# A chunked recurrence with two MLPs behind it: a set order for VectorE, full-height products placed by DMA, relu squared on ScalarE

## The chip, the cores and the metric

The kernel runs on one NeuronCore of a Trainium2 chip. The metric is device time of one execution in microseconds; the median of several executions counts. TensorE (PE) multiplies matrices into PSUM, VectorE (DVE), ScalarE (ACT) and GpSimd (POOL) work elementwise, and SyncE (SP) issues most of the DMAs. Each engine works through its own instructions in order and waits on semaphores for the others.

## What is computed

Three parts follow each other. First a recurrence over 768 steps for 4 batches of 8 heads with a 40 x 40 state each; then a dense MLP whose activation is relu squared; then a mixture of 8 experts with one expert per token. All in float32. The cores of the first two:

```python
for t in range(S):
    y[:, :, t] = np.einsum('bhd,bhde->bhe', rt, state)
    Sa = np.einsum('bhde,bhe->bhd', state, at)
    state_decay = state * wt[:, :, None, :] - np.einsum('bhd,bhe->bhde', Sa, bt)
    state = state_decay + np.einsum('bhd,bhe->bhde', vt, kt)

h = x @ w_in
r = np.maximum(h, 0.0)
g = r * r
return (g @ w_out).astype(np.float32)
```

The third part takes the argmax of x @ w_gate for each token, gives the token to that expert's relu MLP (320 to 1024 to 320) and scales by the softmax weight.

## The kernel before, in words

The 768 steps are cut into 12 superchunks of 64 (index s), each of two chunks of 32 (index c). Inside a chunk the recurrence is turned into matrix products and the inverse of unit lower triangular 32 x 32 matrices. The MLP of a superchunk (a "burst", 8 pieces fp of up product, activation and down product) is cut into pieces that are laid between the recurrence's steps, so that TensorE has something to do while the recurrence waits for other engines. The experts come last, from about 800 us on.

What a superchunk needs is made ahead. `scale` (line 143) loads the decays w and the operands k, b and a of a superchunk, and `products` (line 115) forms running products of w: r by a backward scan (line 126), a clamp (line 135) after ScalarE has looked at the range (line 133), a reciprocal seed, and q by a forward scan (line 139). kb is multiplied by r (line 158) and a by q (through `times`, line 283). The scans exist twice: 104 rows and 1040 columns for operands with the head's columns on partitions (buffers w_d and rq16), and 128 rows and 650 columns in `steps` (line 230, buffers wl and rq10) for operands with the steps on partitions. Both share one seed buffer, seed_q. `by_step` transposes r and q into rt and qt.

`lower` (line 175) makes the products pa of a and kb; ScalarE copies one half to ab (line 186), VectorE masks the other half to am (line 188) and transposes it into a (line 192). `invert` (line 195) transposes ab to al (line 199), and then GpSimd alone works through 31 dependent pairs of a product and a subtraction (line 290: tmp, then tl). tmp shares its one buffer with am. `inverted` (line 215) transposes tl to tf and makes tt from it, which `solve` needs in the next superchunk.

A chunk runs through slots (lines 1430 to 1484): slot_a `out` of the chunk before (products py, and y by VectorE, line 389; ScalarE doubles the last 64 columns, line 390) and `right` (pr); slot_b `add_y` (line 463 and 464: y transposed by TensorE to pt and split into x_hi, x_lo, x_mx for the MLP), `solve` (psa, with ScalarE's copies to sa and zv), in the first chunk of a superchunk also `lower` and `invert` for the superchunk after, and the transposes pz of `other`; slot_d the transposes psd and the products ppq; slot_e, in the first chunk, `steps` of the next superchunk; slot_f `mix`, in the first chunk `decay` of the operands of the next superchunk (line 349), and `fetch`, the loads for the next chunk and the product of zk with rx (line 283); slot_g the update pn of the state (line 307). After each slot MLP pieces are taken, as many as `SLOTS` says: 18 in the first chunk, 14 in the second. `up` (line 647) makes relu on ScalarE (line 654), its square gh on ScalarE (line 658), and on VectorE the product of pl and g (line 659) and the rest gl (line 660). The down product reads gh and gl two pieces later.

A planner orders each engine's instructions from this program order, a timing model and priorities, and so may draw an instruction ahead whose inputs are there. `issue_after` sets an order by hand on one engine; `behind` puts VectorE's instructions behind the last state update in that way. Tiles of a tag share its buffers: rx and the range check's output share one, al and tf share one (solve).

Of the kernel before, what the change touches and what calls it, by code (L numbers as in the profile page):

```python
# [28 lines left out]
SC = 64  # L29
NS = S // SC  # L30
C = 32
# [41 lines left out]
class Rwkv:  # L73
# [6 lines left out]
    def __init__(self, ctx, tc, ps, consts, keep, wd, kb, ad, rv, wl, tok, vt, rng, cst):  # L80
# [28 lines left out]
        self.sums = []  # L109
# [8 lines left out]
    def products(self, w, n, rows, name):  # L118
# [16 lines left out]
        nc.vector.tensor_scalar(out=rf, in0=rf, scalar1=1.0 / LIM, scalar2=LIM, op0=ALU.max, op1=ALU.min)  # L135
        nc.vector.reciprocal(out=self.sq[:rows, 0:n, 0], in_=r[:rows, :, 0])
        yield r
        q = self.tile([128, n, SEG], f"rq{n}.q{name}", 1)
        nc.vector.tensor_tensor_scan(out=q.rearrange("p a b -> p (a b)")[:rows], data0=w[:rows, 0:L],  # L139
                                     data1=seed,  # L140
                                     initial=0.0, op0=ALU.mult, op1=ALU.add)
        yield q

    def scale(self, s):

        nc, src = self.nc, self.src
        w, kb, a = self.w, self.kb, self.a[s % 2]
# [1206 lines left out]
def tile_rwkv__mlp__moe(ctx, tc, wd, kb, ad, rv, wl, tok, vt, nat, w_in, w_out, w_gate, w1, w2, cap, cst1, cst2, cst3, out):  # L1354
# [9 lines left out]
    with ExitStack() as ph:  # L1364
# [24 lines left out]
        with tc.high_priority(offset=AHEAD):  # L1389
# [3 lines left out]
            for _ in rw.scale(1):  # L1393
                pass
# [225 lines left out]
```

## Time and profile before

| | |
|---|---|
| median of 3 executions | 1119.45 us (1116.76 to 1121.55) |
| the profiled execution | 1115.53 us, of it 1113.7 us from the first to the last instruction |
| TensorE, weight loads | 906.6 and 854.7 us busy |
| VectorE | 848.5 us busy |
| ScalarE | 565.9 us busy |
| GpSimd | 510.4 us busy |
[...]

Busy time is not progress: matmuls overlap, and a slow clock makes the same matmuls longer. The busy sums are averages over the load of the weights (up to about 220 us), the superchunks, and the experts. In the rows below, a line such as "POOL tmp <- DVE a L192" names the waiting instruction's output and line first, then what ended the wait. A group "x9 | 6.1, 680 | 8.1 <-ACT gh" has the count, the busy microseconds, the mean of one in nanoseconds, and the idle time ahead of it.

### The profile page before, as it was taken

Reading aid. Unit: us, or ns where it says so; the run is one execution under the profiler, and the core shown is the slowest. Engines: PE = TensorE matmul, PEld = TensorE weight load, DVE = VectorE, ACT = ScalarE, POOL = GpSimd, SP = SyncE. Lnnn points to the kernel's source line nnn. Section 1 sums busy time; section 2 is a strip of 40 time slices with the busy share of each in tenths; the row PEclk is TensorE's granted clock in tenths of the full one; section 3 lists DMA queues with packets and bytes.
Section 4 is the critical chain, followed back from the end, with each engine's and each line's share of the span. In section 5 each row is a group of like instructions: output and inputs, shape, how many; then the busy total and the mean of one; then the engine's idle time right before and its main releaser. Section 6 shows DMA issues by size and latency. Waiting matters only on the chain.

```text
span 1113.7 us, 38734 instructions
## 1 busy us (share of the span) xinstructions
PE 906.6 (81%) x15962; PEld 854.7 (77%) x15962; DVE 848.5 (76%) x1807; ACT 565.9 (51%) x1546; POOL 510.4 (46%) x866
## 2 busy tenths in 40 slices
PE   1645348798898988898979888999899998999992
PEld 1544337688787878887969787899799998989992
DVE  7978888687787877978777878764777878778860
ACT  2434435454544544545454545555273667767750
POOL 4692763848383828284746557540000132223220
PEclk9755558888999989898998999999899999999997
DMA  8833544854444444454535444343294576768720
GB/s 212 252 92 102 153 113 118 275 137 129 116 135 134 134 129 132 123 151 106 156 103 141 121 132 136 103 125 83 74 315 117 160 224 195 224 199 237 216 81 9
DMA packets 86111, 164.18 MB, mean 147 GB/s; under 512 B 15709, under 2 KB 46047, under 8 KB 84960
## 3 DMA queue, kind: packets, MB, share of 16 engines
q1 hardware_dynamic: 76848, 141.52, 45.1%
q10 hardware_dynamic: 6192, 11.06, 3.6%
q0 software_dynamic: 2880, 8.98, 2.5%
q8 instruction: 129, 2.11, 0.9%
q14 instruction: 62, 0.51, 0.2%
HBM read 137.34 MB, written 16.24 MB: 138 GB/s over the span
## 4 chain that ended last, share of the span: by engine, by line
PE 40%; DVE 18%; DMA 12%; POOL 11%; issue 10%; ACT 3%; SPq 0%; POOLq 0%; DVEq 0%; ACTq 0%
PE pl L448 12%; PE acc L632 11%; DMA out_dram<-uo,room 6%; POOL tl L290 5%; POOL tmp L290 5%; DMA xg<-x_dram,room 3%; PE upl L448 3%; PE uacc L1142 3%; PE ppq L293 2%; DVE rq_r L126 2%; PE pn L293 2%; DVE a L283 2%; DVE rq_q L139 1%; DVE zk L283 1%; PE psa L293 1%
## 5 line engine op out<-in xcount | busy, mean ns | idle before, releaser
L290 POOL TENSOR_TENSOR tmp<-solve_al,tl 128x126 f32<-128x126 f32 (+22 forms) x372 | 188.1, 506 | 211.3 <-DVE a L192 183.1
L290 POOL TENSOR_TENSOR tl<-tl,tmp 128x126 f32<-128x126 f32 (+22 forms) x372 | 220.0, 592 | 29.1
L632 PE MATMUL acc<-woh,gh 128*128 128x328 f32 x384 | 129.5, 343 | 2.3 <-ACT x L685 1.9
L659 DVE TENSOR_TENSOR g<-pl,g 128x512 f32<-128x512 f32 x96 | 65.6, 684 | 84.5 <-ACT gh L658 83.6
L448 PE MATMUL pl<-x_hi,wi_hi 128*128 128x256 f32 x384 | 122.3, 318 | 6.5 <-DVE g L659 3.4
L632 PE MATMUL acc<-wol,gh 128*128 128x328 f32 x384 | 123.0, 326 | 0.0
L448 PE MATMUL pl<-x_lo,wi_hi 128*128 128x256 f32 x384 | 115.6, 301 | 8.1 <-DVE x_lo L463 8.1
L448 PE MATMUL pl<-x_hi,wi_lo 128*128 128x256 f32 x384 | 114.6, 298 | 0.0
L654 ACT ACTIVATE g<-pl 128x512 f32<-128x512 f32 x96 | 57.4, 598 | 94.7 <-PE pl L448 93.6
L1220 POOL DMA_INDIRECT out_dram<-uo,room x30 | 34.1, 1137 | 149.9 <-DVE uo L1209 82.4
L1150 POOL DMA_INDIRECT xg<-x_dram,room x30 | 30.7, 1022 | 147.1 <-DVE room L982 66.7
L632 PE MATMUL acc<-woh,gl 128*128 128x328 f32 x384 | 92.4, 323 | 0.0
L448 PEld LDWEIGHTS pl<-x_hi,wi_hi 128*128 128x128 f32 x384 | 79.8, 208 | 10.0 <-DVE g L659 3.5
L448 PEld LDWEIGHTS pl<-x_lo,wi_hi 128*128 128x128 f32 x384 | 80.5, 210 | 8.4 <-DVE x_lo L463 8.4
L1142 PE MATMUL uacc<-w2h,hh 128*128 128x320 f32 x240 | 76.6, 319 | 9.6 <-DVE uo L1209 9.4
L632 PEld LDWEIGHTS acc<-woh,gh 128*128 128x128 f32 x384 | 76.4, 199 | 4.9 <-ACT x L685 2.2
L448 PEld LDWEIGHTS pl<-x_hi,wi_lo 128*128 128x128 f32 x384 | 80.0, 208 | 0.0
L632 PEld LDWEIGHTS acc<-wol,gh 128*128 128x128 f32 x384 | 76.9, 200 | 0.5 <-issue 0.5
L1142 PE MATMUL uacc<-w2h,hl 128*128 128x320 f32 x240 | 75.0, 312 | 0.0
L1142 PE MATMUL uacc<-w2l,hh 128*128 128x320 f32 x240 | 74.9, 312 | 0.0
L403 ACT COPY zk<-pz 40x160 f32<-40x160 f32 x184 | 52.8, 287 | 34.3 <-PE pz L271 31.6
L660 DVE TENSOR_TENSOR gl<-g,gh 128x512 fp32r<-128x512 f32 x96 | 67.9, 707 | 1.8
(266 smaller groups left out, 2716.3 us busy)
## 6 DMA issues: line engine op xcount, KB each, us to landing
wol<-wol SPq DMA_DIRECT2D x96, 328.0 KB
w<-in_w_dram SPq DMA_DIRECT2D x30, 640.0 KB
w<-in_w_dram SPq DMA_DIRECT2D x30, 512.0 KB
zv<-in_vt_dram SPq DMA_DIRECT2D x48, 208.0 KB
kb_d<-in_kb_dram SPq DMA_DIRECT2D x24, 320.0 KB
zk<-in_tok_dram SPq DMA_DIRECT2D x48, 160.0 KB
rx<-rt SPq DMA_DIRECT2D x192, 40.0 KB
w<-in_w_dram SPq DMA_DIRECT2D x30, 256.0 KB
```

What stands on the lines that cost most here:

```text
L283: self.nc.vector.tensor_tensor(op=ALU.mult, **k)
L290: self.last = f(*a, **k).ins
L293: self.tc.keep_in_program_order(self.nc.tensor.matmul(*a, **k))
L403: self.nc.scalar.copy(v[:, y], pz[j][one(y)[1]])
L448: tc.keep_in_program_order(tc.nc.tensor.matmul(out, lhsT=a, rhs=b, start=n == 0, stop=n == len(seq) - 1))
L632: self.tc.keep_in_program_order(self.nc.tensor.matmul(*a, **k))
L654: nc.scalar.activation(g, pl, AF.Relu)
L659: nc.vector.tensor_tensor(out=g, in0=pl, in1=g, op=ALU.mult)
L660: self.behind = (square, nc.vector.tensor_tensor(out=gl, in0=g, in1=gh.bitcast(F32), op=ALU.subtract).ins)
L1142: self.tc.keep_in_program_order(self.nc.tensor.matmul(*a, **k))
L1150: nc.gpsimd.indirect_dma_start(out=xg[:, 0:DX], out_offset=None, in_=self.x1, in_offset=bass.IndirectOffsetOnAxis(ap=self.idx[2 * j + t], ...
L1220: self.nc.gpsimd.indirect_dma_start(out=self.out, out_offset=bass.IndirectOffsetOnAxis(ap=self.to[:, n:n + 1], axis=0), in_=o[:, t], in_of ...
```

## The change

- `up`: ScalarE squares relu in place into g and copies it to gh; VectorE's product of pl and g goes.
- The a operand is loaded into one tile of 104 rows, ax, that shares rq16's one buffer with r; it is multiplied by q in one product of 104 rows, read there by pa, and copied into the two halves of a by DMAs on SP (`place`), the second chunk at once and the first after its decay, which is one product of 104 rows too.
- k and b by steps are loaded into a tile tk of 128 rows in `fetch`; `ready`, in slot_b of the next chunk, multiplies it by rx in one product, and two DMAs place the halves in zk.
- The q scans write over w instead of a buffer of their own. The clamp comes ahead of the range check, whose limits move to 2/LIM and LIM/2.
- `gated` puts VectorE's instructions behind those listed in `gate`: the last one of `add_y` (x_mx), and from `invert` on al. It holds for the r scans of both kinds, am, the product in `ready` and the decay of a, from superchunk 2 on (`steady`).
- In `scale` the products start two slots later; am and its transposes move to `put`, after `invert`.
- tmp has a buffer of its own. ab shares one with sad instead.
- The doubled last 64 columns of y are made by a second VectorE product from py instead of ScalarE's copy from y.

```diff
+        nc.vector.tensor_scalar(out=rf, in0=rf, scalar1=1.0 / LIM, scalar2=LIM, op0=ALU.max, op1=ALU.min)
         if n == 10:
             s = name
 
                 over = self.tile([128, n, SEG], f"over.{s}_{k}", 1, tag="rx")
                 nc.scalar.activation(over, r, AF.Relu,
                                      bias=self.c["lim"][:, k:k + 1], scale=sign, accum_out=self.rng[:, k, s:s + 1])
-        nc.vector.tensor_scalar(out=rf, in0=rf, scalar1=1.0 / LIM, scalar2=LIM, op0=ALU.max, op1=ALU.min)
         nc.vector.reciprocal(out=self.sq[:rows, 0:n, 0], in_=r[:rows, :, 0])
         yield r
-        q = self.tile([128, n, SEG], f"rq{n}.q{name}", 1)
-        nc.vector.tensor_tensor_scan(out=q.rearrange("p a b -> p (a b)")[:rows], data0=w[:rows, 0:L],
-                                     data1=seed,
+        q = w[:, 0:L]
+        nc.vector.tensor_tensor_scan(out=q[:rows], data0=q[:rows], data1=seed,
                                      initial=0.0, op0=ALU.mult, op1=ALU.add)
-        yield q
+        yield q.rearrange("p (a b) -> p a b", a=n)
...
     def scale(self, s):
 
         nc, src = self.nc, self.src
-        w, kb, a = self.w, self.kb, self.a[s % 2]
+        w, kb = self.w, self.kb
         for j in range(2):
             nc.sync.dma_start(out=w[BY_COL[j]], in_=src["wd"][s, j])
         for j in range(2):
             nc.sync.dma_start(out=kb[BY_COL[j]], in_=src["kb"][s, j])
 
+        yield
+        yield
         pr = self.products(w, 16, ROWS, s)
-        r = next(pr)
+        with self.gated():
+            r = next(pr)
         yield
         for k in range(2):
             with self.behind(2):
                 nc.vector.tensor_mul(kb[:ROWS, k], kb[:ROWS, k], r[:ROWS, :, 1:SEG])
-            yield
+        yield
         g = self.tile([128, 16], f"g64.{s}", 2)
         nc.vector.tensor_copy(g[:ROWS], r[:ROWS, :, 0])
         self.pre[s] = [g, [None] * NC, None]
-        for j in range(2):
-            nc.sync.dma_start(out=a[BY_COL[j], :, j].rearrange("p c n t -> p c (n t)"), in_=src["ad"][s, j])
+        x = self.tile([128, NC, 16, C], f"rq16.a{s}", 1)
+        nc.sync.dma_start(out=x[:ROWS].rearrange("p c n t -> p (c n t)"), in_=src["ad"][s])
         q = next(pr)
-        yield
-        for j in range(2):
-            v = a[BY_COL[j], :, j]
-            with self.behind(2):
-                self.times(s > 0 or j == 0, out=v, in0=v, in1=q[BY_COL[j], :, 0:SC].rearrange("p n (c t) -> p c n t", c=NC))
+        with self.behind(2):
+            nc.vector.tensor_tensor(out=x[:ROWS], in0=x[:ROWS], in1=q[:ROWS, :, 0:SC].rearrange("p n (c t) -> p c n t", c=NC),
+                                    op=ALU.mult)
+        self.ax = x
+        self.place(s, 1)
         self.wl = self.tile([128, 1 + 10 * SEG], f"wl.{s}", 1)
         nc.sync.dma_start(out=self.wl, in_=src["wl"][s])
         yield
 
+    def place(self, s, c):
+
+        for j in range(2):
+            self.nc.sync.dma_start(out=self.a[s % 2][BY_COL[j], c, j], in_=self.ax[BY_COL[j], c])
+
     def lower(self, s, c):
         kb, a = self.kb, self.a[s % 2][:, c]
+        if s == 0 and c == 0:
+            self.place(s, 0)
         if c == 0:
-            self.ab = self.tile([128, C, NC, H], f"ab.{s}", 1)
+            self.ab = self.tile([128, C, NC, H], f"sad.ab{s}", 1)
         pa = self.psum(f"pa{s}_{c}").rearrange("p (h k s) -> p h k s", h=H, k=2)
         t0 = c * C
         for h, b, i, lane, ty, j in heads():
             rows = BY_COL[j]
-            self.mm(pa[lane, h], lhsT=a[rows, j, i], rhs=kb[rows, :, i, t0:t0 + C], start=True, stop=True)
+            self.mm(pa[lane, h], lhsT=self.ax[rows, c, i], rhs=kb[rows, :, i, t0:t0 + C], start=True, stop=True)
         nc.scalar.copy(self.ab[:, :, c, :], pa[:, :, 1, :].rearrange("p h s -> p s h"))
+        self.todo.append((s, c, a, pa))
+
+    def put(self):
+
+        nc = self.nc
+        s, c, a, pa = self.todo.pop(0)
         am = self.tile([128, H, C], f"am.{s}_{c}", 1)
-        nc.vector.tensor_tensor(out=am, in0=pa[:, :, 0, :], in1=self.c["mlow"][:, None, :].to_broadcast([128, H, C]),
-                                op=ALU.mult)
+        with self.gated():
+            nc.vector.tensor_tensor(out=am, in0=pa[:, :, 0, :], in1=self.c["mlow"][:, None, :].to_broadcast([128, H, C]),
+                                    op=ALU.mult)
         for j in range(2):
             ak = a[BY_STEP[j], j].rearrange("p (h y) t -> p y h t", y=2)
             nc.vector.transpose(out=ak[:, 0], in_=am[BY_STEP[j]])
...
+        i = nc.vector.transpose(out=al.rearrange("p s t -> p (s t)"), in_=self.ab.rearrange("p s c h -> p s (c h)")[:, :, None].to_broadcast([128, C, 2, NC * H]))
+        self.gate = [i.ins]
         tl = self.tile([128, C, C // 2], f"tl.{s}", 1)
-        tmp = self.tile([128, 144], f"tmp.{s}", 1, tag="am")
+        tmp = self.tile([128, 144], f"tmp.{s}", 1)
...
     def steps(self, s):
 
         pr = self.products(self.wl, 10, 128, s)
-        r = next(pr)
+        with self.gated():
+            r = next(pr)
         yield
...
-        for j in range(2):
-            nc.sync.dma_start(out=zk[BY_STEP[j], j], in_=src["tok"][s, c, j])
+        tk = self.tile([128, 16, D], f"tk.{s}_{c}", 1)
+        nc.sync.dma_start(out=tk.rearrange("p n e -> p (n e)"), in_=src["tok"][s, c])
...
+        self.got.append((zk, tk, rx))
+
+    def ready(self):
+
+        nc = self.nc
+        if not self.got:
+            return
+        zk, tk, rx = self.got.pop(0)
+        v = tk.rearrange("p (h y) e -> p y h e", y=2)
+        with self.gated():
+            nc.vector.tensor_tensor(out=v, in0=v, in1=rx, op=ALU.mult)
         for j in range(2):
-            v = zk[BY_STEP[j], j].rearrange("p (h y) e -> p y h e", y=2)
-            self.times(c == 1 or s > 0, out=v, in0=v, in1=rx[BY_STEP[j]])
+            nc.sync.dma_start(out=zk[BY_STEP[j], j], in_=tk[BY_STEP[j]])
...
+    def gated(self):
+
+        order = ExitStack()
+        for i in self.gate if self.steady else ():
             order.enter_context(self.tc.issue_after(i))
...
     def decay(self, s):
 
-        g = self.pre[s][0]
-        for z in (self.a[s % 2][:, 0], self.zv[0]):
-            for j in range(2):
-                v, w = z[BY_COL[j], j], g[BY_COL[j], :, None].to_broadcast([D, 16, C])
-                if z is self.zv[0]:
-                    v = each(v)
-                    w = g[BY_COL[j]].rearrange("p (n y) -> p n y", y=2)[:, :, :, None].to_broadcast([D, 8, 2, D])
-                self.nc.vector.tensor_mul(v, v, w)
-            yield
+        g, x = self.pre[s][0], self.ax[:ROWS, 0]
+        with self.gated():
+            self.nc.vector.tensor_mul(x, x, g[:ROWS, :, None].to_broadcast([ROWS, 16, C]))
+        self.place(s, 0)
+        yield
...
+        self.nc.vector.tensor_mul(y[:, 0:DM], py, q)
+        self.nc.vector.tensor_mul(y[:, DM:], py[:, DM - 64:], q[:, DM - 64:])
...
-        square = nc.scalar.activation(gh, g, AF.Square).ins
-        nc.vector.tensor_tensor(out=g, in0=pl, in1=g, op=ALU.mult)
-        self.behind = (square, nc.vector.tensor_tensor(out=gl, in0=g, in1=gh.bitcast(F32), op=ALU.subtract).ins)
+        nc.scalar.activation(g, g, AF.Square)
+        self.behind = (nc.scalar.copy(gh, g).ins, nc.vector.tensor_tensor(out=gl, in0=g, in1=gh.bitcast(F32), op=ALU.subtract).ins)
...
-        lim=np.broadcast_to([[1.0 / LIM, -LIM]], (128, 2)),
+        lim=np.broadcast_to([[2.0 / LIM, -LIM / 2]], (128, 2)),
...
-                        ml.add_y(xs[last[0]], last[1], y)
+                        rw.gate = [ml.add_y(xs[last[0]], last[1], y).ins]
...
+                        rw.put()
+                        rw.put()
                     if c == 0 and s > 0:
                         next(decay)
                     others(0)
+                    rw.ready()
...
+                rw.steady = s > 1
```

Left out: the host's layouts of a and of k and b by steps (now 104 and 128 rows in one piece), returned instructions, a renamed tag for a late tile of the experts, and the calls of `put` and `ready` for superchunk 0.

## Rows read from the trace of the kernel before

**Rows 1.** Busy time by stretch: length, then PE, PEld, DVE, ACT, POOL, clock, DMA.

```profile
222.00:281.00 59.00, 53.38 (x1158) 49.69 (x1158) 49.54 (x80) 29.88 (x75) 38.55 (x68) 0.86 0.47 128
...
637.00:696.00 59.00, 50.28 (x1166) 47.01 (x1166) 47.15 (x78) 29.18 (x73) 34.71 (x65) 0.94 0.51 140
696.00:745.00 49.00, 47.03 (x1153) 44.21 (x1153) 32.87 (x60) 27.29 (x68) 26.20 (x62) 0.97 0.41 112
745.00:793.00 48.00, 47.72 (x1004) 45.35 (x1000) 29.32 (x75) 24.85 (x62) 0.00 (x0) 1.00 0.28 80
```

**Rows 2.** Who waited for whom: us in total, times, longest.

```profile
POOL tmp L290 <- DVE a L192: 183.1, 12, 21.6
...
PE psd L271 <- DVE x_mx L464: 26.0, 9, 4.1
...
PE pz L271 <- DVE x_mx L464: 20.5, 8, 3.7
...
DVE rq_r L135 <- ACT over L133: 19.7, 10, 2.4
```

**Rows 3.** Timeline of VectorE at one superchunk's head: start, length.

```profile
398.48 0.48 DVE L389 TENSOR_TENSOR y<-py,qt 128x320 f32<-128x320 f32 x1
398.88 2.31 DVE L126 TENSOR_TENSOR_SCAN rq_r<-w_d,seed_q 104x1040 f32<-104x1040 f32 x1
...
406.50 0.27 DVE L464 TENSOR_TENSOR x_mx<-pt,tops 64x128 fp32r<-64x128 f32 x1
...
408.62 1.23 DVE L199 STREAM_TRANSPOSE solve_al<-ab 128x1024 f32<-128x1024 f32 x1
```

**Rows 4.** Busy time by stretch, right behind that head.

```profile
407.00:413.00 6.00, 6.00 (x30) 5.92 (x29) 5.83 (x13) 3.33 (x9) 0.00 (x0) 0.51 0.63 148
```

**Rows 5.** Timeline of GpSimd: two inversions, first and last steps, one slow step.

```profile
413.32 0.24 POOL L290 TENSOR_TENSOR tmp<-solve_al,tl 128x31 f32<-128x31 f32 x1 [17.95 <-DVE a L192]
...
427.78 3.56 POOL L290 TENSOR_TENSOR tl<-tl,tmp 128x128 f32<-128x128 f32 x1
...
450.96 0.22 POOL L290 TENSOR_TENSOR tl<-tl,tmp 128x16 f32<-128x16 f32 x1
...
706.54 0.24 POOL L290 TENSOR_TENSOR tmp<-solve_al,tl 128x31 f32<-128x31 f32 x1 [13.92 <-DVE a L192]
...
737.29 0.22 POOL L290 TENSOR_TENSOR tl<-tl,tmp 128x16 f32<-128x16 f32 x1
```

**Rows 6.** VectorE's groups in superchunk 5 (398 to 459 us).

```profile
L659 DVE TENSOR_TENSOR g<-pl,g 128x512 f32<-128x512 f32 x9 | 6.1, 680 | 8.1 <-ACT gh L658 8.0
...
L283 DVE TENSOR_TENSOR zk<-zk,rx 64x640 f32<-64x640 f32 x4 | 3.4, 847 | 1.7 <-DMA zk<-in_tok_dram 1.6
...
L283 DVE TENSOR_TENSOR a<-a,rq_q 40x1024 f32<-40x1024 f32 x2 | 2.7, 1338 | 0.0
L158 DVE TENSOR_TENSOR kb_d<-kb_d,rq_r 104x1024 f32<-104x1024 f32 x2 | 2.3, 1208 | 0.0
...
L349 DVE TENSOR_TENSOR a<-a,g 40x512 f32<-40x512 f32 x2 | 1.4, 686 | 0.0
```

**Rows 7.** ScalarE's group of squares in superchunk 5.

```profile
L658 ACT ACTIVATE gh<-g 128x512 fp32r<-128x512 f32 x8 | 5.0, 630 | 0.2
```

**Rows 8.** The chain that ended last, two DMA pieces: start, length.

```profile
253.81 3.59 DMA a<-in_ad_dram
...
390.39 4.68 DMA rx<-rt
```

**Rows 9.** Timeline: al and GpSimd's first step, first and third inversion.

```profile
33.85 1.24 DVE L199 STREAM_TRANSPOSE solve_al<-ab 128x1024 f32<-128x1024 f32 x1
...
38.34 2.52 POOL L290 TENSOR_TENSOR tmp<-solve_al,tl 128x31 f32<-128x31 f32 x1 [1.72 <-DVE a L192]
...
179.63 1.24 DVE L199 STREAM_TRANSPOSE solve_al<-ab 128x1024 f32<-128x1024 f32 x1
...
182.74 0.24 POOL L290 TENSOR_TENSOR tmp<-solve_al,tl 128x31 f32<-128x31 f32 x1 [21.57 <-DVE a L192]
```

More of the change, by code (lines that the diff above doesn't have):

```diff
@@ L108, in __init__ @@
         self.last = None
-        self.sums = []
+        self.todo, self.got = [], []
+        self.sums, self.gate, self.steady = [], [], False
         self.pre, self.rt = {}, {}
@@ L198, in invert @@
         al = self.tile([128, C, C], f"solve.al{s}", 1)
-        nc.vector.transpose(out=al.rearrange("p s t -> p (s t)"), in_=self.ab.rearrange("p s c h -> p s (c h)")[:, :, None].to_broadcast([128, C, 2, NC * H]))
+        i = nc.vector.transpose(out=al.rearrange("p s t -> p (s t)"), in_=self.ab.rearrange("p s c h -> p s (c h)")[:, :, None].to_broadcast([128, C, 2, NC * H]))
+        self.gate = [i.ins]
         tl = self.tile([128, C, C // 2], f"tl.{s}", 1)
-        tmp = self.tile([128, 144], f"tmp.{s}", 1, tag="am")
+        tmp = self.tile([128, 144], f"tmp.{s}", 1)
         eng, pin = nc.gpsimd, self.pool
@@ L276, in behind @@
         for i in self.sums[:n]:
+            order.enter_context(self.tc.issue_after(i))
+        return order
+    def gated(self):
+        order = ExitStack()
+        for i in self.gate if self.steady else ():
             order.enter_context(self.tc.issue_after(i))
@@ L340, in decay @@
     def decay(self, s):
-        g = self.pre[s][0]
-        for z in (self.a[s % 2][:, 0], self.zv[0]):
-            for j in range(2):
-                v, w = z[BY_COL[j], j], g[BY_COL[j], :, None].to_broadcast([D, 16, C])
-                if z is self.zv[0]:
-                    v = each(v)
-                    w = g[BY_COL[j]].rearrange("p (n y) -> p n y", y=2)[:, :, :, None].to_broadcast([D, 8, 2, D])
-                self.nc.vector.tensor_mul(v, v, w)
-            yield
+        g, x = self.pre[s][0], self.ax[:ROWS, 0]
[3 more added lines that the diff above has]
+        yield
+        for j in range(2):
+            v = each(self.zv[0][BY_COL[j], j])
+            w = g[BY_COL[j]].rearrange("p (n y) -> p n y", y=2)[:, :, :, None].to_broadcast([D, 8, 2, D])
+            self.nc.vector.tensor_mul(v, v, w)
+        yield
     def turn(self, s, c):
@@ L382, in out @@
     def out(self, s, c):
-        py = self.psum(f"py{s}_{c}")[:, 0:DM].rearrange("p (h e) -> p h e", h=H)
+        py = self.psum(f"py{s}_{c}")[:, 0:DM]
+        ph = py.rearrange("p (h e) -> p h e", h=H)
         for h, b, i, lane, ty, j in heads():
             rows = BOTH[j]
-            self.mm(py[lane, h], lhsT=self.lr[c][rows, j, i], rhs=self.zk[c][rows, j, i], start=True, stop=True)
+            self.mm(ph[lane, h], lhsT=self.lr[c][rows, j, i], rhs=self.zk[c][rows, j, i], start=True, stop=True)
         y = self.tile([128, DM + 64], f"y.{s}_{c}", 1)
-        self.nc.vector.tensor_mul(y[:, 0:DM].rearrange("p (h e) -> p h e", h=H), py, self.pre[s][1][c])
-        self.nc.scalar.copy(y[:, DM:], y[:, DM - 64:DM])
+        q = self.pre[s][1][c].rearrange("p h e -> p (h e)")
+        self.nc.vector.tensor_mul(y[:, 0:DM], py, q)
+        self.nc.vector.tensor_mul(y[:, DM:], py[:, DM - 64:], q[:, DM - 64:])
         return y
@@ L1020, in early @@
         nb, n = 2 * FIRST_UNITS, 2 * NE
-        op = [rw.tile([128, m, 128], f"{t}.op{m}", 1, dt=F32R) for t, m in (("solve", 8), ("rq16", 8), ("ab", n - 16))]
+        op = [rw.tile([128, m, 128], f"{t}.op{m}", 1, dt=F32R) for t, m in (("solve", 8), ("rq16", 8), ("sad", n - 16))]
         ov = rw.tile([128, n, nb], "rq10.ov", 1, dt=F32R)
@@ L1448, in slot_b @@
                         rw.invert(s + 1)
+                        rw.put()
+                        rw.put()
                     if c == 0 and s > 0:
@@ L1451, in slot_b @@
                     others(0)
+                    rw.ready()
                 def slot_c():
@@ L1561, in layouts @@
     kb = np.stack([by_col(k), by_col(b)], axis=3)
-    ad = by_chunk(a).transpose(0, 1, 2, 4, 3, 5)
+    ad = np.zeros((NS, ROWS, NC, 16, C), np.float32)
+    for j in range(2):
+        ad[:, BY_COL[j]] = by_chunk(a).transpose(0, 1, 2, 4, 3, 5)[:, j]
     rv = np.stack([by_chunk(x).transpose(0, 4, 1, 2, 3, 5) for x in (r, v)], axis=2)
```

8 lines of the change are left out of this document (4 added, 4 removed).

## The prediction, made before the changed kernel was run

> **What bounds the kernel now.** First I read the busy time by stretch, cut at every second y product, so that a row is one superchunk [rows 1]. Eight rows, for superchunks 2 to 9, run alike from 222 to 696 us: 474 / 8 = 59.25 us each, of which TensorE shows 50 to 53 us and VectorE 47 to 49.5. The row of superchunk 10 is the one to look at: nothing is left to load and scale two superchunks ahead, VectorE's sum falls from 47.15 to 32.87 us, and the stretch falls from 59 to 49 us though TensorE does nearly the same work. Superchunk 11 takes 48. So TensorE would go through a superchunk in some 49 us, and about 10 us of each of the eight are lost because VectorE comes late.
>
> Where, the waits tell [rows 2]: TensorE stands for x_mx, the last piece of add_y, at the transposes of both chunks (psd, pz), for up to 4.1 us at once. VectorE's timeline of one head shows why [rows 3]: y is made at 398.48, x_mx only at 406.50; between them VectorE, which works in order, does the 104-row scan (2.31 us), clamps, zk products and state products that nobody needs yet. Behind x_mx it starts al at 408.62. [...]
>
> Then GpSimd: it runs the inversion from 413.32 to 451.18 us, 37.9 us, and before that stood 17.95 us [rows 5]. What ended the stand is the transpose of am, not al: al was ready at 408.62 + 1.23 = 409.85, 3.5 us earlier, but tmp shares its buffer with am. That is so 12 times [rows 2].
>
> **The change part by part, per superchunk.**
> (1) ScalarE squares relu. Eight products g <- pl,g of 0.680 us leave VectorE: 5.4 us [rows 6]. ScalarE gets a copy more per piece; its row is bounded below by nothing gained and above by the square's 0.630 us [rows 7], which has the same shape, so I take that: 5.0 us on an engine busy 29 of 59 us [rows 1]. Beside other work. The path from pl to gh grows by 0.6 us, but the down product that reads gh is two pieces behind; without that cover it would cost 8 x 0.6 = 5 us.
> (2) Full-height products. The a products, 2 x 1.338 us, become one of the kb product's width, 1.208: 1.5 us. The decay of a, 2 x 0.686, becomes one: 0.7 us. Four zk products of 0.847 become two, of the same length per lane: 1.7 us [rows 6]. Sum 3.9 us. The y tail moves from ScalarE's copy to VectorE: a 64-column product, twice, under the 0.27 us of x_mx's 64 x 128 form [rows 3], costs up to 0.5; it takes ScalarE's turn out of the path to the transposes.
> (3) Waits that go: the clamp no longer waits for ScalarE's two range sums (19.7 us over 10, 2.0 each, [rows 2]); the zk product no longer waits for a load that had to wait for py (1.6 us in this superchunk, [rows 6]). The load now goes to tk, which py doesn't read.
> (4) Placing: two SBUF-to-SBUF DMAs for each a half and each zk, eight more issues on SP against three loads fewer. What one takes is bounded by nothing seen below and by the slowest rx <- rt piece, 4.68 us [rows 8], above. Both placed operands are read by TensorE long after (a when the next superchunk starts, zk at the update that ends the chunk), so I cost them at nothing; without that cover it is one 4.68 per chunk, 9.4 us.
> (5) Order. At the superchunk's head x_mx is followed by al; am, the decay of a and the zk product are queued behind al, the 104-row scan behind x_mx of the second chunk. Queued behind the waiting instructions are rt's transposes and the second chunk's fetch, and later the a products, which pa reads; see the second rival.
> (6) tmp's own buffer: the inversion starts 3.5 us earlier.
>
> VectorE loses 5.4 + 3.9 - 0.5 = 8.8 us of work and 2.0 + 1.6 us of waits, but the second wait shows in some superchunks only (I count half): 11.6. When superchunk 10 lost 14.3 us of VectorE work it became 10.3 us shorter than the mean, 0.72 of it. The same share gives 8.3 us, a superchunk of 50.9. The inversion's loop is a second bound: 59.25 - 37.9 = 21.4 us now pass between its end and its next start; 3.5 go with the buffer, and of the 10.1 us from y to al [rows 3] I take 4 off, since 2.31 of scan and some 3.5 of zk, decay and clamp are no longer in them but ScalarE still has to copy ab after zv. 37.9 + 13.9 = 52 us. The later one holds: 52, 7.25 us less, times eight 58 us.
>
> **Before 222 us** the inversion heads the chain of waits; three of them start behind am: 3.25 us late at the first (33.85 + 1.24 against 38.34), 1.9 at the third [rows 9]. Three times about 2.7 is 8 us. That the weights' decoding also gains from a freer VectorE is the upper end: two superchunks' 3.9 and one burst's 5.4, 13 us; I don't take it, since GpSimd is what the chain runs through there. **After 696 us** TensorE is busy 47 of 49 and 48 of 48 us [rows 1]: 1 us each. The experts' part is untouched.
>
> Sum: 58 + 8 + 2 = 68 us. The profiled execution took 1115.53 us (1.8 outside its span), 3.9 under the median of 1119.45; taken off the median, 1051 us.
>
> [...] GpSimd's steps, 0.4 to 0.5 us mostly, stretch to 3.56 us at 427.78 [rows 5], in the middle of VectorE's kb products. From 706.54 to 737.51, with no such work about, the whole inversion takes 31.0 us instead of 37.9. [...]
>
> **Rivals.**
> *GpSimd becomes the bound.* The 104-row scan (2.31) and the 65-column one that stood in the head move into the inversion: about 3.8 us more, 41.7 + 13.9 = 55.6 us a superchunk; 29 + 10 off: 1080. For: the 6.9 us of difference above. Against: a and zk products shrink in the same stretch. Chance 0.2.
> *The products come late for pa.* The 104-row scan now runs in the second chunk only, and the a load waits for its buffer (it shares rq16's), so scan 2.31, clamp 0.7, kb 2.4, load 3.59 [rows 8], product 1.2 follow each other: 10.2 us, plus some 8 of other VectorE work, in a second chunk of 14 of 32 pieces, 23 us, less the 3 to x_mx. That leaves 2. TensorE works in order: while pa waits for ax, pz and the next pl stand too. It turns into a loss from 7.25 us of lateness; at 10, 62 us a superchunk, +22 - 10: 1131. For it: the a buffer was double and loaded early. Against: the load runs beside the q scan. Chance 0.07.
> *All head waits go.* The eight run at 49 us like the last two: 82 + 10: 1027, and with the 13 us of decoding 1014. Chance 0.2.
> *VectorE's time is given back.* The code's own order of pieces leaves TensorE standing at psa and zv instead, and the change doesn't get its order where other ungated products slip in; only GpSimd's 3.5 us, or nothing: 1091 down to 1119. Chance 0.08.
>
> **How the numbers follow.** The forecast has 0.45. Measurements of this kernel tell some 0.5%, 5.6 us, from no change. Faster: 0.45 + 0.2 + 0.2 and 0.04 of the last, 0.89; same 0.04; slower 0.07. The range goes from the lowest case, 1014, to the upper end of the last rival's gaining half, 1091: outside are 0.07, the rest of the last rival 0.04 and some 0.05 below.
>
> **What would show it.** Right: VectorE near 38 us in a superchunk row, ScalarE near 33; x_mx within 4 us of y in both chunks; GpSimd's first step within 0.3 us of al's end; psd and pz no longer waiting for x_mx; superchunks of 51 to 53 us. The first rival: GpSimd's run over 40 us and tf waiting for it. The second: pa standing for ax. Wrong altogether: rows of 57 us or more, or a first part up to 222 us that grew.

## The result and the profile after

The changed kernel took 1075.2 us in the median of 4 executions (1068.5 to 1081.4), beside 1119.1 us of the kernel before on the same chip: ratio 0.9605, 95% interval 0.957 to 0.964. That is faster, by 44 us where 68 were forecast: 24 us above the predicted number, inside its range.

The profiled execution took 1074.91 us, 1073.1 of it from the first to the last instruction, 40.6 less than before. Cut at the y products, superchunks 2 to 9 gave 37.2 of it (472.9 us before, 435.7 now, 54.5 each), the part before them 4.6 (222.8 to 218.2); superchunks 10 and 11 and the experts cost 0.5 and 0.7 more. VectorE's busy time fell from 848.5 to 753.3 us, ScalarE's rose from 565.9 to 620.8, TensorE's mean granted clock from 0.888 to 0.946 of full speed. That rise is no result of the change: in a later series the kernel before had 0.880 at 1116.2 us and 0.936 at 1115.9.

Busy time by stretch, changed kernel (superchunks 3, 6, 10 and 11; columns as in [rows 1]):

```profile
273.01:325.83 52.82, 50.71 (x1158) 47.94 (x1159) 38.86 (x68) 33.82 (x80) 36.56 (x66) 0.90 0.63 166
435.07:491.26 56.19, 52.53 (x1166) 49.09 (x1166) 38.95 (x67) 33.92 (x80) 36.81 (x66) 0.88 0.59 155
653.89:703.34 49.45, 46.95 (x1123) 44.35 (x1125) 30.91 (x64) 34.30 (x81) 30.07 (x65) 0.97 0.51 143
703.34:752.17 48.83, 48.36 (x1061) 45.95 (x1047) 26.09 (x77) 29.84 (x69) 0.00 (x0) 1.00 0.39 106
```

VectorE has 38.9 us a superchunk and ScalarE 33.9, as worked out. The last two superchunks are as long as before. The others differ among themselves, from 50.9 to 56.6 us.

The waits of the changed kernel, against [rows 2]:

```profile
POOL tmp L326 <- DVE solve_al L216: 98.3, 11, 18.6
...
POOL tl L326 <- DVE solve_tf L238: 41.0, 11, 6.9
...
DVE solve_al L216 <- ACT sad_ab L196: 30.8, 10, 5.6
...
PE pt L494 <- DVE y L428: 24.2, 8, 8.6
...
DVE rq_a L170 <- DMA rq_a<-in_ad_dram: 18.6, 11, 3.2
...
PE psd L300 <- DVE x_mx L503: 3.4, 2, 2.2
```

GpSimd's wait for the next inversion has nearly halved (183.1 us before), while its wait for tf, ahead of it in the same pause, has grown from 21.6 to 41.0. pz no longer appears behind x_mx, and psd only twice. Two waits are new: al for ScalarE's copy ab, and VectorE itself for a's load. TensorE's wait at the transposes of y has grown from 15.9 to 24.2.

VectorE around the head at 435 us (against [rows 3]), from x_mx of the chunk before (rq_a is the tile ax in the profile's names):

```profile
416.17 0.27 DVE L503 TENSOR_TENSOR x_mx<-pt,tops 64x128 fp32r<-64x128 f32 x1
...
417.25 2.39 DVE L127 TENSOR_TENSOR_SCAN rq_r<-w_d,seed_q 104x1040 f32<-104x1040 f32 x1
...
428.14 2.04 DVE L343 TENSOR_TENSOR zv<-zv,pn 40x320 f32<-40x320 f32 x4
432.20 1.23 DVE L170 TENSOR_TENSOR rq_a<-rq_a,w_d 104x1024 f32<-104x1024 f32 x1 [2.02 <-DMA rq_a<-in_ad_dram]
433.34 1.24 DVE L238 STREAM_TRANSPOSE solve_tf<-tl 128x1024 f32<-128x1024 f32 x1
...
435.07 0.48 DVE L428 TENSOR_TENSOR y<-py,qt 128x320 f32<-128x320 f32 x1
...
438.28 0.27 DVE L503 TENSOR_TENSOR x_mx<-pt,tops 64x128 fp32r<-64x128 f32 x1
444.17 1.25 DVE L216 STREAM_TRANSPOSE solve_al<-sad_ab 128x1024 f32<-128x1024 f32 x1 [5.61 <-ACT sad_ab L196]
```

x_mx follows y after 3.2 us instead of 8.0. But a's product stands 2.02 us for its load, and tf, which ends the inversion for TensorE, is queued behind it on VectorE, y behind tf. GpSimd (against [rows 5]) and the issues on SP in the same stretch:

```profile
430.35 0.22 POOL L326 TENSOR_TENSOR tl<-tl,tmp 128x16 f32<-128x16 f32 x1
434.64 0.53 POOL L326 MEMSET tl<- 128x512 f32 x1 [4.07 <-DVE solve_tf L238]
...
445.56 0.24 POOL L326 TENSOR_TENSOR tmp<-solve_al,tl 128x31 f32<-128x31 f32 x1 [9.99 <-DVE solve_al L216]
```

```profile
423.49 4.01 SPq L284 DMA_DIRECT2D rx<-rt  x5
427.60 0.49 SPq L167 DMA_DIRECT2D rq_a<-in_ad_dram  x1
```

GpSimd is done at 430.57 and tf starts at 433.34, 2.8 us later: GpSimd is not what tf waits for. The load's buffer, that of r, was read for the last time by the copy to g (422.95 + 0.33), but its issue sits on SP behind five pieces of rx. (Whether an earlier issue would take the stand away was not tried.) At the other end the own buffer works: the first step at 445.56 is 0.14 us behind al's end (444.17 + 1.25).

Right behind the head the clock is 0.50, beside 0.51 in [rows 4], over a stretch that now holds the short matmuls of psa and pa; TensorE had stood 2.08 us for y just ahead of it:

```profile
438.00:444.00 6.00, 4.97 (x173) 4.46 (x165) 0.56 (x3) 2.64 (x7) 0.00 (x0) 0.50 0.33 89
```

What such a clock costs shows in the kernel before: one product of pl (128x256) lasts 0.41 us at 0.50 (407 to 412.6 us) and 0.28 at 1.00 (413.1 to 420 us).

### The profile page after: what moved, and what is told of

It is laid out like the page before. It is cut to its first block, busy times and chain, and to the rows that moved or that the text cites. A ratio compares the mean times of both kernels' runs of the same rounds, so it can differ in the third digit from the quotient of the medians.

```text
span 1073.1 us, 38714 instructions
## 1 busy us (share of the span) xinstructions
PE 901.4 (84%) x15962; PEld 852.6 (79%) x15962; DVE 753.3 (70%) x1691; ACT 620.8 (58%) x1618; POOL 516.4 (48%) x863
## 3 DMA queue, kind: packets, MB, share of 16 engines
q8 instruction: 129, 2.11, 0.9%
## 5 line engine op out<-in xcount | busy, mean ns | idle before, releaser
L326 POOL TENSOR_TENSOR tmp<-solve_al,tl 128x126 f32<-128x126 f32 (+22 forms) x372 | 202.9, 546 | 126.5 <-DVE solve_al L216 98.3
L487 PE MATMUL pl<-x_hi,wi_hi 128*128 128x256 f32 x384 | 118.6, 309 | 0.5 <-ACT x_hi L499 0.5
L487 PE MATMUL pl<-x_lo,wi_hi 128*128 128x256 f32 x384 | 112.6, 293 | 4.1 <-DVE x_lo L502 2.6
L487 PE MATMUL pl<-x_hi,wi_lo 128*128 128x256 f32 x384 | 112.2, 292 | 0.0
L1180 PE MATMUL uacc<-w2h,hh 128*128 128x320 f32 x240 | 76.5, 319 | 11.6 <-DVE uo L1247 11.4
L487 PEld LDWEIGHTS pl<-x_lo,wi_hi 128*128 128x128 f32 x384 | 76.9, 200 | 4.6 <-DVE x_lo L502 2.9
L487 PEld LDWEIGHTS pl<-x_hi,wi_hi 128*128 128x128 f32 x384 | 76.6, 199 | 3.6 <-ACT x_hi L499 0.9
L487 PEld LDWEIGHTS pl<-x_hi,wi_lo 128*128 128x128 f32 x384 | 76.7, 200 | 0.0
L671 PEld LDWEIGHTS acc<-woh,gl 128*128 128x128 f32 x384 | 68.9, 199 | 2.4 <-DVE gl L698 2.4
L329 PE MATMUL pa<-kb_d,rq_a 40*32 40x64 f32 x1536 | 38.3, 277 | 34.2 <-DVE rq_a L170 27.2
```

The source lines that it names most:

```text
L326: self.last = f(*a, **k).ins
L329: self.tc.keep_in_program_order(self.nc.tensor.matmul(*a, **k))
L487: tc.keep_in_program_order(tc.nc.tensor.matmul(out, lhsT=a, rhs=b, start=n == 0, stop=n == len(seq) - 1))
L671: self.tc.keep_in_program_order(self.nc.tensor.matmul(*a, **k))
L1180: self.tc.keep_in_program_order(self.nc.tensor.matmul(*a, **k))
```

## The experiments

All runs first, in one table. The last four columns are in us and come from one profiled execution of each kernel: the mean of superchunks 2 to 9 (from y to y), and for the inversions made in them the mean of GpSimd's run (first step to last), of its pause until the next first step, and of how long after GpSimd's end VectorE starts tf.

| kernel | ratio to before, 95% interval | superchunk | run | pause | tf behind |
|---|---|---|---|---|---|
| before | 1 | 59.1 | 38.5 | 20.3 | 1.1 |
| changed | 0.9605 (0.957 to 0.964) | 54.5 | 40.6 | 13.8 | 3.3 |
| before_tmp | 0.9981 (0.9948 to 1.0015) | 59.0 | 38.6 | 19.7 | 3.5 |
| before_sq | 0.9868 (0.9815 to 0.9921) | 56.5 | 39.6 | 16.9 | 1.3 |
| before_order | 1.0082 (1.0048 to 1.0117) | 59.4 | 39.8 | 19.8 | 8.8 |
| after_nosq | 0.9713 (0.9645 to 0.9781) | 55.4 | 39.7 | 15.6 | 4.4 |
| after_nogate | 1.0108 (1.0048 to 1.0169) | 60.9 | 39.2 | 20.9 | 6.0 |
| gate_al | 0.9741 (0.9646 to 0.9836) | 55.7 | 41.2 | 14.4 | 3.4 |
| gate_mx | 0.9558 (0.9477 to 0.9638) | 54.1 | 36.2 | 18.1 | 5.0 |
| after_short | one execution, 1046.5 us | 53.3 | 24.7 | 28.3 | 18.3 |
| a_behind_y | 0.9535 (0.9477 to 0.9592) | 52.6 | 40.4 | 12.2 | 0.6 |
| behind_y_mx | 0.9461 (0.9394 to 0.9528) | 52.2 | 36.9 | 15.7 | 0.4 |
| pages_good | 0.9447 (0.9401 to 0.9493) | 52.5 | 40.5 | 12.1 | 0.5 |
| pages_bad | 0.9597 (0.9542 to 0.9652) | 53.6 | 40.5 | 13.3 | 0.4 |

**Single parts on the kernel before.** Own buffer alone, ScalarE's square alone:

```diff
-        tmp = self.tile([128, 144], f"tmp.{s}", 1, tag="am")
+        tmp = self.tile([128, 144], f"tmp.{s}", 1)
```

> The kernel before with a buffer of its own for GpSimd's products, nothing else. The prediction's term: the inversion starts 3.5 us earlier in the superchunks and some 2.7 us earlier in three early ones. If the inversion's end decides when tf comes, 8 x 3.5 + 8 = up to 36 us: 1083. Theory 'VectorE is late anyway': tf follows the state update on VectorE and not the inversion's end in most superchunks, so only the early three count: 1109 to 1114 us.

Measured: no difference that can be told. GpSimd now starts 0.1 us behind al, but VectorE has not come further, so tf starts 3.5 us behind GpSimd's end instead of 1.1: what was gained at the front is lost again at the back. Only the first part gained, 222.8 to 219.2 us.

```diff
-        square = nc.scalar.activation(gh, g, AF.Square).ins
-        nc.vector.tensor_tensor(out=g, in0=pl, in1=g, op=ALU.mult)
+        nc.scalar.activation(g, g, AF.Square)
...
```

> The kernel before with relu squared on ScalarE, nothing else: 5.4 us a superchunk off VectorE, 5 us on ScalarE. If VectorE's work counts by 0.72 as the prediction's share says, 8 x 3.9 = 31 us: 1088. Theory 'only the head counts': the g products mostly lie outside the head (one of eight in it), so 1 us a superchunk or less: 1108 to 1119 us.

Measured: 1.3% or 15 us, between the two. 2.6 us of the 5.4 us taken off VectorE reach each superchunk, half of them, not 0.72.

In the changed kernel the same edit undone:

> The changed kernel with VectorE's product of pl and g back and ScalarE's copy gone, nothing else. By the 0.72 share it loses 31 us: 1106. If only the head counts, VectorE has room at 38 us of 54 and it loses 8 us or less: 1075 to 1083 us.

Measured: the square is worth 0.0108 there, 12 us. That is more than the 8 us of the second case and far from the 31 of the first: the other parts keep most of the gain.

**The order and the work, each without the other.** before_order is the kernel before with the order set on VectorE and tmp's own buffer, all its work left on VectorE:

```diff
+        with self.gated():
+            r = next(pr)
...
+        self.todo.append((s, c, a, pa))
...
+                        rw.gate = [ml.add_y(xs[last[0]], last[1], y).ins]
...
+                        rw.put()
+                        rw.put()
...
+                    rw.ready()
```

> The kernel before with part 5 and 6 of the change alone: VectorE's order at the superchunk's head (x_mx, then al, then am, the decay of a and the zk products; the 104-row scan behind x_mx of the second chunk) and tmp's own buffer. All of VectorE's work stays: eight g products, narrow products, the clamp behind ScalarE's range sums. If the order alone carries the gain: ratio 0.965 to 0.975, as with the g products back in the changed kernel (0.9713). If order and lighter VectorE are needed together: 0.98 to 1.00, since VectorE's 47 to 49 us only move to other places in the superchunk.

after_nogate is the changed kernel with nothing held back on VectorE; the program order, with am behind `invert` and the products two slots later, stays:

```diff
-                rw.steady = s > 1
+                rw.steady = False
```

> The changed kernel without the order set on VectorE at the superchunk's head (what was held behind al or x_mx is free to be placed by the planner). If the order carries a good part of the gain: psd and pz stand for x_mx again, superchunks of 56 to 58 us, ratio 0.975 to 0.985. If the gain is in the work taken off VectorE alone: within 5 us of the changed kernel's 0.9605.

Measured: each half alone makes the kernel slower, by 0.8% and 1.1%; together they make it 4% faster. Both are outside what I expected. Rows of each show where the time goes. VectorE and then GpSimd of before_order:

```profile
504.60 2.47 DVE L309 TENSOR_TENSOR a<-a,rq_q 40x1024 f32<-40x1024 f32 x2
507.10 1.00 DVE L333 TENSOR_TENSOR zv<-zv,pn 40x320 f32<-40x320 f32 x2
...
509.66 1.23 DVE L230 STREAM_TRANSPOSE solve_tf<-tl 128x1024 f32<-128x1024 f32 x1
```

```profile
502.96 0.22 POOL L316 TENSOR_TENSOR tl<-tl,tmp 128x16 f32<-128x16 f32 x1
510.95 0.53 POOL L316 MEMSET tl<- 128x512 f32 x1 [7.77 <-DVE solve_tf L230]
```

The head is as wished, but what was put behind it runs in the second chunk: from x_mx there (491.20) to tf (509.66) VectorE works through 18.5 us without a gap, and tf comes 6.5 us after GpSimd's end. zv stands behind a's products there, and TensorE's pr waits for it (50.2 us over the run). VectorE of after_nogate, at a head whose y was at 412.08:

```profile
420.76 0.82 DVE L295 TENSOR_TENSOR tk<-tk,rx 128x640 f32<-128x640 f32 x1 [2.61 <-DMA tk<-in_tok_dram]
421.55 2.33 DVE L127 TENSOR_TENSOR_SCAN rq_r<-w_d,seed_q 104x1040 f32<-104x1040 f32 x1
423.79 1.22 DVE L216 STREAM_TRANSPOSE solve_al<-sad_ab 128x1024 f32<-128x1024 f32 x1
```

Here the product of a chunk to come stands for its load in front of al, and the scan follows it. a's product, too, stands 42.4 us over 11 for its load, more than twice the 18.6 of the changed kernel. That VectorE has less to do than in the kernel before was worth nothing here, while what it stood for lay ahead of what others waited for: GpSimd stood 144.5 us over 11 for al, against 98.3 in the changed kernel.

**Which half of the order.** The changed kernel, held behind al alone or behind x_mx alone:

```diff
-                        rw.gate = [ml.add_y(xs[last[0]], last[1], y).ins]
+                        ml.add_y(xs[last[0]], last[1], y)
```

> The changed kernel with only the half of the order that holds am, the decay of a, the zk product and the 128-row scan behind al; nothing is held behind x_mx in the second chunk, so the 104-row scan and what follows it come earlier, in the first chunk. If al's place is what counts: ratio 0.955 to 0.965, superchunks of 52 to 55 us. If x_mx of the second chunk counts as much: psd and pz stand for it in that chunk, 0.975 to 0.99.

```diff
-        self.gate = [i.ins]
+        i.ins
```

> The changed kernel with only the other half: what is held back is held behind x_mx, not behind al. Ahead of al stand then the zk product with its wait for a load, the 128-row scan, the decay of a, a clamp and am: some 4.6 us. If al's place is what counts, GpSimd starts some 4.6 us later and superchunks grow by 3 to 5 us: ratio 0.98 to 1.00. If not, it stays at 0.9605 within 0.005.

Measured: gate_mx keeps the whole gain. gate_al loses a third of it, by its interval between a tenth and six tenths, and its ratio lies between my two ranges. My expectation of gate_mx was wrong. al does have the zk product, both scans and a clamp ahead of it, but in the changed kernel VectorE stood 5.61 us there for ab, and part of these fit in: in one head al starts 9.92 us after y (434.56 to 444.48), against 9.10 in the changed kernel, and in the mean of eight heads 9.9 against 7.5, 2.4 later instead of 4.6. GpSimd's run is shorter for it, 36.2 us instead of 40.6 (for what goes with that, see the rivals below). In the first of the eight superchunks tf came 15.9 us behind GpSimd's end; the other seven have 3.4. gate_al, VectorE in the second chunk (its profiled execution took 1100.0 us beside a median of 1088.4, so I read waits from it and not the lengths in the table):

```profile
473.62 0.27 DVE L503 TENSOR_TENSOR x_mx<-pt,tops 64x128 fp32r<-64x128 f32 x1
486.49 1.23 DVE L170 TENSOR_TENSOR rq_a<-rq_a,w_d 104x1024 f32<-104x1024 f32 x1 [12.60 <-DMA rq_a<-in_ad_dram]
```

The planner put a's product right behind x_mx, and VectorE stood 12.6 us for the load; over the run 82.2 us over 11. psd stands for x_mx only twice there, 3.8 us in all, and al starts no later after y than in the changed kernel (6.9 us in the mean). So the rows point at this product's place; no run of its own separates it here.

**What tf waits for.** a's product put behind y; GpSimd's run cut to 21 of its 31 steps:

```diff
-        with self.behind(2):
+        yield
+        yield
+        with self.behind(2), self.after_y():
...
+    def after_y(self):
+        return self.tc.issue_after(self.made) if self.steady else ExitStack()
...
+        self.made = self.nc.vector.tensor_mul(y[:, DM:], py[:, DM - 64:], q[:, DM - 64:]).ins
```

> The changed kernel with its a product put behind y on VectorE (and traced two slots later), nothing else. Theory 'late load': in the changed kernel the a product stands some 2 us for its load right after the state update, and tf, y and tt stand behind it; so here y comes some 4 us sooner after the update, TensorE does not stand for y, and the eight superchunks fall from 54.5 to 50-52 us: 1040 to 1055 us. Rival 'GpSimd bound': the loop is the inversion's run of 40.7 us and its fixed pause; tf comes at most 2 us sooner, superchunks 53-54: 1062 to 1073 us. Rival 'late for pa': the product now comes too late for pa and the gain is given back: 1070 us or more.

```diff
-        for j in range(C - 1):
+        for j in range(C - 11):
```

> The changed kernel with 21 of GpSimd's 31 steps (the last ten pairs left out; what is computed differs, the time of the superchunks up to some 750 us is what is read). GpSimd's run falls from 40.6 to about 31 us. If GpSimd bounds the loop, superchunks 2 to 9 fall from 54.5 to 50 or below. If tf is late because a's product stands for its load on VectorE ahead of it (late load), GpSimd only stands longer: superchunks of 53.5 to 55 us.

Measured: with the product out of the way tf starts 0.6 us behind GpSimd's end instead of 3.3, and superchunks fall by 1.9 us to 52.6: 0.7% faster than the change, with intervals that just overlap. That lies between my cases: tf comes as much sooner as 'late load' says, but the time of 1062.4 us is in the range of the rival 'GpSimd bound'. With GpSimd 15.9 us shorter per run, and the product left where it was, superchunks fall by only 1.1 us, to 53.3, and GpSimd's pause takes nearly all of it:

```profile
413.16 0.53 POOL L326 MEMSET tl<- 128x512 f32 x1 [19.37 <-DVE solve_tf L238]
423.57 0.24 POOL L326 TENSOR_TENSOR tmp<-solve_al,tl 128x31 f32<-128x31 f32 x1 [9.48 <-DVE solve_al L216]
```

So a's product with its late load is what the changed kernel's loop runs through, and GpSimd's run lies just under it; in a_behind_y the two are level. How much of the 1.9 us belongs to the stand and how much to the product itself was not separated. That after_short's span is 28 us shorter in all is mostly the part before superchunk 2 (201.5 us against 218.2), where GpSimd does bound.

**Both together.** a_behind_y held behind x_mx only, for a version that beats both kernels:

```diff
-        self.gate = [i.ins]
+        i.ins
```

> a_behind_y (a's product behind y) together with gate_mx (what was held behind al is held behind x_mx only, some 4.6 us of VectorE's work may stand ahead of al). In the changed kernel al waits 3 us a superchunk for ScalarE's copy ab anyway, so gate_mx cost nothing there. In the short superchunks of a_behind_y (49.9 to 50.3 us) al waits only 0.5 us. If the loop through GpSimd (its run of 40.5 us and 9.6 us of pause) sets their length, al comes 3 to 4 us later in those, and they become 52 to 54 us: ratio 0.957 to 0.970 against 0.9535 of a_behind_y. If VectorE's list in the second chunk sets the length, moving work to the head shortens it: ratio 0.945 to 0.9535.

Measured: 0.9461, in the second range, but for a reason in neither; its interval overlaps that of a_behind_y. The pause did grow by 3.5 us, as the first case says, and the run fell by as much. GpSimd and tf of behind_y_mx in one superchunk:

```profile
436.86 0.24 POOL L331 TENSOR_TENSOR tmp<-solve_al,tl 128x31 f32<-128x31 f32 x1 [12.81 <-DVE solve_al L218]
...
473.81 0.22 POOL L331 TENSOR_TENSOR tl<-tl,tmp 128x16 f32<-128x16 f32 x1
```

```profile
474.06 1.25 DVE L240 STREAM_TRANSPOSE solve_tf<-tl 128x1024 f32<-128x1024 f32 x1
```

The run is 37.2 us, and tf starts 0.03 us behind its end in 7 of 8: here GpSimd's loop, 36.9 + 15.7, is the bound, and it beats the changed kernel by 1.4%. Of the 13 us by which its profiled span is shorter than a_behind_y's, 4 lie before the experts; why the experts' part took 313.4 us instead of 322.8 was not tried, so most of the difference between these two has no known cause.

**Why heads of the same kernel differ.** Even in a_behind_y superchunks take 49.9 to 56.2 us with the same instructions. Stretches of a long and a short one, and TensorE in the head of each:

```profile
425.54:480.53 54.99, 51.71 (x1169) 48.78 (x1168) 39.12 (x68) 33.84 (x80) 36.74 (x65) 0.91 0.58 157
536.70:586.62 49.92, 47.93 (x1164) 44.55 (x1163) 38.67 (x68) 33.70 (x80) 36.60 (x65) 1.00 0.65 177
```

```profile
426.56 0.64 PE L334 MATMUL psa<-rh,tt 32*32 32x40 f32 x27
429.46 0.77 PE L334 MATMUL psa<-rh,tt 32*32 32x40 f32 x37 [2.26 <-issue]
430.16 2.58 PE L334 MATMUL pa<-kb_d,rq_a 40*32 40x64 f32 x90
433.76 1.28 PE L334 MATMUL pa<-kb_d,rq_a 40*32 40x64 f32 x38 [1.02 <-issue]
...
537.72 1.12 PE L334 MATMUL psa<-rh,tt 32*32 32x40 f32 x64
538.76 0.86 PE L334 MATMUL pa<-kb_d,rq_a 40*32 40x64 f32 x45
539.89 1.42 PE L334 MATMUL pa<-kb_d,rq_a 40*32 40x64 f32 x83 [0.27 <-issue]
```

In the long head TensorE stands 2.26 and 1.02 us for nothing that the profile shows ("issue"), 37 + 90, that is some 128, matmuls apart, and its clock is lower afterwards: 0.50 from 433 to 439 us, against 1.00 from 541 to 547 behind the short head. The profile page's list of DMA queues has one that carries instructions:

```profile
q8 instruction: 129, 2.11, 0.9%
```

129 packets of 16 KB; the 15962 matmuls and as many weight loads make 247 to a packet, if it brings TensorE's alone (an estimate from these counts). That the stands wait for these packets can be read from the traces: in the 14 of them, from 10 us ahead of superchunk 2 to the end of superchunk 10, TensorE has 142 stands of more than 0.15 us put to "issue", and each ends 1.1 to 1.9 us after a packet of this queue has ended, half of them within 1.3 to 1.5 us, while such packets come about nine to a superchunk. From one superchunk to the next the place of the stand moves 22 matmuls ahead. To move it otherwise, 42 products of `inner` were computed once more in superchunks 3, 5, 7 and 9 (and 33 in superchunk 1 for pages_bad):

```diff
-        for h, b, i, lane, ty, j in heads():
+        for h, b, i, lane, ty, j in (list(heads()) * 3)[:32 + PADS.get((s, c), 0)]:
...
-AHEAD = 5000
+AHEAD, PADS = 5000, {(3, 1): 42, (5, 1): 42, (7, 1): 42, (9, 1): 42}
```

> The kernel of a_behind_y (a's product behind y) with 42 of chunk 1's inner products computed a second time in superchunks 3, 5, 7 and 9: 84 records of matmul and weight load more each, same values, 1.5 us of TensorE each. Instruction theory: in the trace of a_behind_y TensorE stands, for nothing that the profile shows, in the run of short matmuls at the head of a superchunk, always 128 records apart, and the places move 22 records ahead per superchunk: after record 115, 93, 71, 49, 27, 4, 110, 88 of the run for superchunks 2 to 9. The instruction queue brings packets of 16 KB. Where one place falls between 88 and 115 the superchunk took 49.9 to 52.1 us, where it falls at 71 to 4 it took 53.5 to 56.2. The extra records move the places of superchunks 4 to 7 and 10 into 92 to 115: these four superchunks fall from 53.5-56.2 to 50-52 us, with 3 us less in superchunk 10, total ratio 0.940 to 0.945. Rival (the long heads come from the loads or from ScalarE's copies, not from where the instructions are cut): long and short superchunks stay as they were, 5 to 6 us of work more, ratio 0.957 to 0.960.

> As pages_good, and 33 inner products once more in superchunk 1 (66 records): the places then fall after records 49 and 27 in turn for superchunks 2 to 10. Instruction theory: every superchunk from 2 to 9 takes 53.5 to 55.5 us, ratio 0.963 to 0.975, 25 us or more over pages_good though the work differs by 1 us. Rival (not from where the instructions are cut): within 3 us of pages_good.

Measured: the places went where they were put. In pages_bad the stands of superchunks 2 to 9 came after 42, 27, 48, 25, 46, 24, 45 and 22 matmuls of the run, or 128 further on (49 and 27 in turn were forecast); one such head:

```profile
593.36 0.54 PE L334 MATMUL psa<-rh,tt 32*32 32x40 f32 x22
596.02 0.95 PE L334 MATMUL psa<-rh,tt 32*32 32x40 f32 x42 [2.12 <-issue]
596.91 2.56 PE L334 MATMUL pa<-kb_d,rq_a 40*32 40x64 f32 x86
600.70 1.49 PE L334 MATMUL pa<-kb_d,rq_a 40*32 40x64 f32 x42 [1.23 <-issue]
```

The two kernels differ by 1.5% in time with 1 us of difference in work; TensorE's order is the same but for the repeated products, while the planner swapped some neighbours on VectorE, ScalarE and SP. Of the 17.4 us between their profiled spans 9.5 lie in superchunks 2 to 9. In pages_good superchunks 4 to 7 fell from 53.5-56.2 to 50.4-52.6 us, nearly as forecast, superchunk 10 not at all; but 8 and 9 rose from 50 to 55, since the place before, 128 matmuls ahead, now fell in or right behind the short matmuls of py and pr, and TensorE stood there for 2.4 and 2.3 us. So the sum over superchunks 2 to 9 hardly changed against a_behind_y (419.6 and 420.8 us), and the rest of pages_good's gain lies in parts that this experiment does not explain: its ratio came into the forecast range by luck. pages_bad's superchunks came at 53.6 in the mean, but from 51.9 to 56.5, five of the eight below the forecast 53.5, and its ratio missed the forecast 0.963 to 0.975. Shown is that the place decides where TensorE stands; how long, it does not decide alone.

## Why the prediction came out as it did

*Steps 1, 2, 4, work.* Right as to the engines: VectorE 38.9 and ScalarE 33.9 us a superchunk against "near 38" and "near 33". The placing DMAs stayed hidden in superchunks 2 to 9; in the first chunk of all TensorE stood 11.6 us for one (pr at 42.47 us).

*Step 5, x_mx and al.* x_mx is 3.2 us behind y in the first chunk (within 4 was said), 5.5 in the second (410.72 to 416.17, not within 4, but TensorE hardly waits for it there any more). al did not come 4 us earlier to y but 2.6 in the mean (10.0 to 7.4 us), since it waits for ab. The predicted pause of GpSimd, 13.9 us, was measured as 13.8, and that is partly luck: it started from one pause of 21.4 where the mean was 20.3, both cuts were smaller than forecast (2.7 for 3.5, 2.6 for 4), tf came 2.3 us later behind GpSimd's end, and y 3.4 sooner behind tf.

*Step 6, own buffer.* It starts GpSimd 3.3 us earlier in the head shown and is worth nothing by itself (before_tmp): what GpSimd gains at its start counts only where VectorE takes up its end at once.

*"The later one holds: 52".* This is the step that failed. Of the two bounds, VectorE's share (50.9) and the loop (52), neither held; the superchunk is 54.5. First, the run was taken at 37.9 us (one run; the mean was 38.5), and it is 40.6: the first rival's mechanism (41.7 forecast), for the scans moved into it. VectorE's scans lie beside GpSimd's run for 4.2 us in the kernel before and 7.6 in the changed one. That the moved scans cost the run their whole length, 3.8 us, was an estimate that no run shows: with 3.4 us more of scans beside it the run grew by 2.1. In the sum of run and pause the longer run alone makes up the missing 2.5 us, and by its number the result (1075.2) lies nearer to that rival's 1080 than to 1051; but its sign, tf waiting for GpSimd, is missing, and after_short shows that a shorter run would hardly have helped. Second, and that is what ended last, VectorE has a list of its own in the second chunk, from x_mx to tf, 17.2 us, which includes 2.0 of standing for a's load and 1.2 of a's product. The second rival had seen this list (10.2 + 8 us of some 20) but looked for its price at pa in the next head, where TensorE waits; the price is paid one step earlier, at tf and y, which stand behind the product on VectorE. a_behind_y takes it away and gives back 1.9 of the 2.5 us that were missing.

*Not in the prediction at all* are TensorE's stands at the head for its instructions (together 4.5 us in the worst one of a_behind_y). The kernel before has them too, in superchunks 2, 5, 6 and 7, and one of them in the very head of [rows 3]:

```profile
400.60 1.86 PE L293 MATMUL pa<-kb_d,a 40*32 40x64 f32 x114
404.91 0.42 PE L293 MATMUL pa<-kb_d,a 40*32 40x64 f32 x14 [2.45 <-issue]
...
406.83 0.57 PE L271 MATMUL pz<-ct,zv 40*104 40x40 f32 x7 [1.32 <-DVE x_mx L464]
```

There it cost nothing, since pz behind it waited another 1.32 us for x_mx. Once x_mx comes early, such a stand shows.

*Before 222 us*: 4.6 us instead of 8. The first inversion starts later than before (43.78 against 38.34 us), and what it ends earlier is 0.6 us; the second gains 2.1, the third 4.9. *After 696 us*: nothing instead of 2 us (98.3 us against 97.7 for both).

*The rivals.* The last, VectorE's time given back, is by its time what happens if one of the halves is missing: before_order and after_nogate gain nothing. Its reason shows in part: in before_order pr stands for zv 50.2 us over the run (3.3 in the kernel before), in after_nogate psd for sa 28.7. What VectorE's work beside it costs GpSimd's run can be read between two kernels: with the same instructions the run takes 40.4 us in a_behind_y and 36.9 in behind_y_mx, where the 128-row scans lie in GpSimd's pause and 4.9 us of scans are left beside the run, instead of 7.7. By what means a scan slows GpSimd's steps was not shown.

## What to carry to other kernels

Take work off an engine that works in order, as VectorE does here, and set its order as one change: here each without the other lost, by 0.8% (before_order) and 1.1% (after_nogate), and both together gained 4%. Put a product whose load may be late behind everything that others wait for, and look at the queue in which that load is issued, not only at when its buffer comes free. Where a bound is worked out from two engines, list the third one's instructions between the same two events as well, with their waits.

## What the runs showed of the hardware

The DMA queue that the profile names "instruction" brings 129 packets, 2.11 MB in all, in a_behind_y. In a stretch of short matmuls (psa's 64 in 1.12 us and pa's 128 behind them, 0.86 us for 45) TensorE stands there for 0.2 to 2.5 us, at places some 128 matmuls apart, until 1.1 to 1.9 us after such a packet has ended. I read the places as the borders of packets; in pages_good and pages_bad they went where repeated products put them. These two kernels, in which only a few repeated products moved the places (and some neighbours on other engines), differ by 1.5%, a little over half of it in superchunks 2 to 9.

GpSimd's steps stretch beside VectorE's scans: in before_order a step of 30 elements at 500.44 took 2.15 us, beside the scan of 2.35 us from 500.18, and ended 0.06 us after it; with no scan beside it the same step took 0.25 (behind_y_mx, 473.19 us). Placed in GpSimd's pause, the 128-row scans and what goes with them save 3.5 us of a run of 40.4 (behind_y_mx against a_behind_y).
